# Reordering the opening of a beacon-attention and maxout-FFN kernel: other places for the first loads, casts, masks and copies

## The chip, the cores and the metric

The kernel runs on one core of a Trainium2 chip. A core has five engines, each with its own instruction queue that is worked off in order: TensorE (PE, matrix multiplies and transposes), VectorE (DVE), ScalarE (ACT), GpSimd (POOL) and SyncE (SP, which here only asks for transfers). Transfers between device memory and the on-chip memory (SBUF) run on 16 DMA engines, fed by a queue for each engine that asks: SyncE's, ScalarE's and GpSimd's. TensorE writes to PSUM, from which the other engines copy to SBUF. The metric is the device time in microseconds of one execution.

## The reference

The inputs are q, k and v of 8 batches, 8 heads, 576 positions and 64 dimensions, 16 further "beacon" keys and values for each batch and head, three weights of 512 x 768 and one of 768 x 512, all float32.

```python
k_all = concat([beacon_k, k]);  v_all = concat([beacon_v, v])
scores = (q @ k_all.T) / 8, causal for the ordinary keys, beacons always seen
a = softmax(scores);  attn = a @ v_all
x = attn as [4608 tokens, 512]
h = maximum(maximum(x @ w1, x @ w2), x @ w3)
out = h @ w_out
```

## The kernel before

The work on the attention goes by pairs of heads (four a batch, 32 in all); a "quad" is two pairs. For a pair the queries and keys are turned by TensorE so that the 64 dimensions lie on partitions (queries in `qT`, keys behind 16 beacon columns in `kT`). Keys and values are cut into five tiles of 128 rows, the first with the beacons in its first 16 rows. Scores are computed with keys on partitions, in four groups a pair (`emit_scores`, L503 to L525: matmuls at L514, an exponential by ScalarE at L523). The causal triangle is put to zero afterwards (`emit_masks`): by GpSimd with a select (L542), or by VectorE with a product with the constant `tri` (L540), which GpSimd makes in the step `triangle` (L787, L788). `emit_pv` (L583) multiplies with ones, for the sums, and with the values, for a quad and half of the positions at a time. ScalarE inverts the sums (`invert`), and VectorE multiplies into `xT` (`multiply`, L616).

The FFN of the first 512 tokens runs in half units of 8 matmuls (`mm1_halves`, L638); VectorE copies the first result (L630) or takes the maximum (L632). The step `("ffn", bank, kind)` takes the next half unit of tokens 0 to 255 (kind 0) or 256 to 511 (kind 1), in the order first, second, third weight, three units each. A bank is one of two in `ffn_psum`, one of two in `pv_psum`, or one from a ring of score tiles, which has two places and from the step `widen` on three. A later user of a place waits until the earlier one is emptied.

The order of all work is written out by hand: the list `first_steps` (L901) for the opening, and `loop_steps` after it. Each step appends its instructions to the queues of the engines that it uses, so the list fixes the order on each engine, and engines run against each other by semaphores alone. Steps that matter here:

- `busy n cols`: n spare matmuls on constants (L478). Spare work is also given with `scores` (third number) and `half` (spare transposes, L408).
- `load half p i queue` (L223): queries (i = 0) or keys (i = 1) of the first half of the positions of pair p of batch 0, asked for by the queue named. `cast half` (L231) makes them bf16 on the engine named.
- `load keys 0` (L351): the beacon keys of batch 0. `cast keys 0`, then `turn keys 0` (L360, copies at L366 and L367), then `keys p engine` (L460), which copies the beacon columns of pair p into `kT`.
- `load quad half g h` (L240): queries and keys of half h of quad g of batch 0, as bf16, from GpSimd's queue. `load quad b g` (L249): a whole quad of batch b in the same way. `load w i` (L338): weight i, two transfers from the same queue.
- `half p h ...` (L440, copies at L448) and `whole p ...` (L389, copies at L464 and L453): turn the queries and then the keys of a pair. Pairs from 8 on come in float32 (`load pair`, L206), are cast by GpSimd (`cast pair`, L259) and turned at L398.
- `load v0 t [gate]`: value tile t of batch 0 (L276, L279), asked for by SyncE. `load v b piece [gate]`: three or two tiles of a later batch. With a gate the engine named first writes one element of the tile (L301, L295; L202 for pairs), and SyncE waits for that. `cast v0 t engine` (L328) and `cast v b piece` (L316, GpSimd) make them bf16.

On GpSimd's queue the requests for transfers, the casts, the selects and the small writes stand behind one another, so a request goes out only when all that was listed ahead of it is done. On SyncE a request whose gate is not yet written holds up those behind it.

## Time and profile before

| | us |
|---|---|
| three runs | 284.79, 285.10, 286.19 (median 285.1) |
| the profiled execution's own time | 285.21 |
| its span, first to last instruction | 283.3 |
| busy: TensorE, VectorE, ScalarE, GpSimd | 276.3, 176.5, 154.5, 143.4 |

The mean clock granted to TensorE is 0.998 of full. In the rows of the profile, a line "Lnnn engine operation out<-in" is a group of instructions of one line of the code; in rows ordered by time the first number is the start and the second the length, both in microseconds from the start of the span, and a bracket gives the idle time before the group and what ended it. `quad`, `whole` and `h` are the staged queries and keys, `bk` the beacon keys, `st` the float32 stage of values and pairs, `at_sb` the exponentials. "issue" is time in which the engine waited for nothing that the profile shows.

### The profile page before, as it was taken

How to read it: one execution, taken by the hardware profiler on the slowest of the kernel's cores; microseconds unless marked ns; L12 is line 12 of the kernel's file. 1: busy time of each engine (PE TensorE's matmuls, PEld its weight loads, DVE VectorE, ACT ScalarE, POOL GpSimd, SP SyncE). 2: the span in 40 equal slices, each digit the busy share in tenths (PEclk: the TensorE clock that was granted, in tenths of full speed). 3: DMA queues.
4: the chain of work that ended last, by engine and by line, in shares of the span. 5: the costliest groups of instructions: out<-in, count | busy, mean ns of one | idle time of the engine just before them, and what ended most of it. 6: DMA issues, size and time to landing. Idle time of an engine off the chain costs nothing.

```text
span 283.3 us, 11781 instructions
## 1 busy us (share of the span) xinstructions
PE 276.3 (98%) x5099; PEld 201.5 (71%) x5099; DVE 176.5 (62%) x331; ACT 154.5 (55%) x249; POOL 143.4 (51%) x316
## 2 busy tenths in 40 slices
PE   8999999999999999999999999999999999999995
PEld 7666777757777576768677686767877687757762
DVE  2456777886676765756566666646575665661754
ACT  2876676897563574637464574725765474624000
POOL 4462318898741583758734497508854682400000
PEclk9999999999999999999999999999999999999999
DMA  9999999999978399999999969989999962003004
GB/s 153 168 171 206 223 234 157 247 206 309 211 141 168 45 252 178 171 197 147 189 178 215 236 91 176 166 204 185 217 160 170 163 177 76 2 3 150 2 2 185
DMA packets 118307, 46.27 MB, mean 163 GB/s; under 512 B 107248, under 2 KB 112880, under 8 KB 118256
## 3 DMA queue, kind: packets, MB, share of 16 engines
q1 hardware_dynamic: 111888, 39.20, 75.6%
q0 software_dynamic: 5808, 6.00, 13.0%
q8 instruction: 40, 0.66, 1.1%
q10 hardware_dynamic: 560, 0.33, 0.4%
q14 instruction: 11, 0.09, 0.1%
HBM read 35.13 MB, written 9.44 MB: 157 GB/s over the span
## 4 chain that ended last, share of the span: by engine, by line
PE 91%; DMA 3%; ACT 2%; POOL 1%; DVE 1%; issue 1%; ACTq 0%; POOLq 0%
PE t L700 44%; PE t L726 16%; PE t L583 11%; PE t L514 6%; DMA quad<-in_k_dram 3%; PE pv L478 2%; ACT at_sb L523 2%; PE pv L638 2%; PE sc L514 1%; PE sc L638 1%; PE fps L638 1%; PE t L398 1%; POOL at_sb L542 1%; PE wide L583 1%; PE pv L583 1%
## 5 line engine op out<-in xcount | busy, mean ns | idle before, releaser
L700 PE MATMUL t<-xT,w_sb 64*128 64x288 bf16 (+1 forms) x1008 | 129.6, 285 | 0.0
L700 PE MATMUL t<-xC,wC 64*128 64x288 bf16 (+1 forms) x1008 | 129.6, 285 | 0.0
L523 ACT ACTIVATE at_sb<-t 128x992 bf16<-128x992 f32 (+1 forms) x96 | 82.6, 863 | 42.8 <-PE t L514 37.1
L632 DVE TENSOR_TENSOR hT<-hT,t 128x576 bf16<-128x576 bf16 (+1 forms) x84 | 63.7, 763 | 30.6 <-PE t L700 30.6
L542 POOL TENSOR_SCALAR_AFFINE_SELECT at_sb<-at_sb 128x256 bf16<-128x256 bf16 (+2 forms) x143 | 53.6, 390 | 53.7 <-ACT at_sb L523 41.2
L700 PEld LDWEIGHTS <-w_sb 64*128 64x128 bf16 x1008 | 51.3, 94 | 12.6 <-issue 1.1
L700 PEld LDWEIGHTS <-wC 64*128 64x128 bf16 x1008 | 51.0, 94 | 12.4
L726 PE MATMUL t<-w_out_sb,hT 128*128 128x512 bf16 x210 | 47.9, 380 | 0.0
L681 POOL COPY xC<-xT 64x576 bf16<-64x576 bf16 (+1 forms) x26 | 18.0, 693 | 42.8 <-DVE xT L616 42.5
L630 DVE CAST hT<-t 128x576 bf16<-128x576 f32 (+1 forms) x36 | 27.7, 769 | 14.8 <-PE t L700 14.6
L726 PEld LDWEIGHTS <-hT 128*128 128x128 bf16 x210 | 19.3, 98 | 22.8 <-issue 0.9
L259 POOL CAST p<-st 96x768 bf16<-96x768 f32 x44 | 34.9, 822 | 0.3
L734 DVE COPY y<-t 128x1024 f32<-128x1024 f32 (+1 forms) x20 | 21.8, 1091 | 20.5 <-PE t L726 20.3
L514 PE MATMUL t<-qT,kT 64*128 64x288 bf16 (+4 forms) x288 | 33.1, 279 | 0.0
L616 DVE TENSOR_TENSOR xT<-t,recip 128x288 bf16<-128x288 f32 (+2 forms) x78 | 22.9, 351 | 16.0 <-ACT recip L606 10.7
L604 ACT ACTIVATE lnd<-t 128x288 f32<-128x288 f32 x26 | 10.7, 410 | 36.9 <-PE t L583 36.9
L514 PEld LDWEIGHTS <-kT 64*128 64x128 bf16 x400 | 18.5, 94 | 11.4 <-issue 6.7
L583 PEld LDWEIGHTS <-v_sb 128*32 128x32 bf16 (+1 forms) x1408 | 24.6, 96 | 1.6 <-issue 0.4
L523 ACT ACTIVATE at_sb<-sc 128x736 bf16<-128x736 f32 (+5 forms) x28 | 23.2, 862 | 4.2 <-PE sc L514 4.1
L583 PE MATMUL t<-at_sb,v_sb 128*32 128x96 bf16 (+8 forms) x1144 | 23.3, 228 | 0.0
L316 POOL CAST v_sb<-st 128x1536 bf16<-128x1536 f32 (+2 forms) x21 | 18.4, 894 | 0.6 <-DMA st<-in_v_dram 0.6
L583 PEld LDWEIGHTS <-ones 128*32 128x32 bf16 (+2 forms) x512 | 10.9, 95 | 6.7 <-issue 3.9
(125 smaller groups left out, 220.1 us busy)
## 6 DMA issues: line engine op xcount, KB each, us to landing
out_dram<-y SPq DMA_DIRECT2D x15, 512.0 KB, 4.6
st<-in_q_dram SPq DMA_DIRECT2D x24, 288.0 KB, 5.8
st<-in_k_dram SPq DMA_DIRECT2D x24, 288.0 KB, 6.2
st<-in_v_dram SPq DMA_DIRECT2D x24, 256.0 KB, 5.5
w_sb<-in_moe_w_dram POOLq DMA_DIRECT2D x6, 384.0 KB, 8.9
st<-in_v_dram SPq DMA_DIRECT2D x8, 224.0 KB, 5.1
st<-in_v_dram SPq DMA_DIRECT2D x8, 160.0 KB, 4.7
out_dram<-y SPq DMA_DIRECT2D x5, 256.0 KB, 4.6
```

The lines of the kernel that those rows point to most:

```text
L259: cast(t16.rearrange("p r h d -> p h r d"), st[0:QP, i * NQ2 : (i + 1) * NQ2].rearrange("p (h r d) -> p h r d", h=2, r=QR),)
L316: cast(v_sb[0:n, t:t1].rearrange("p t h d -> p (t h d)"), st[0:n, (t - t_lo) * H * D : (t1 - t_lo) * H * D],)
L514: nc.tensor.matmul(ps[:, e, off : off + q1 - q0], kT[hs, 128 * t : 128 * t + 128], qT[hs, q0:q1], start=True, stop=True, tile_position=(64 ...
L523: nc.scalar.activation(out=both_heads(p, gi), in_=ps[:, :, 0 : g_width(p, gi)], func=AF.Exp, scale=scale)
L542: nc.gpsimd.affine_select(out=view, in_=view, compare_op=ALU.is_ge, fill=0.0, base=x0, pattern=[[0, 2], [1, hi - lo]], channel_multiplier=-1,)
L583: nc.tensor.matmul(ps[bank][32 * j : 32 * j + 32, lo + q0 - qa : lo + qb - qa], lhsT, at_view(PPQ * quad + j // 2, t, j % 2, q0, qb), star ...
L616: nc.vector.tensor_mul(xT[:, 2 * g + part - 1, c0 + ca : c0 + cb], ps[bank][:, lo : lo + cb - ca], recip[:, ca:cb],)
L630: (by_i or by_dve)(h, ps)
L632: nc.vector.tensor_max(h, h, ps)
L700: nc.tensor.matmul(ps[:, e], w[own(e), ct, cols], x, start=(ct == 0 and not over), stop=(ct == n_ct - 1 and over), tile_position=(64 * e, 0),)
L726: nc.tensor.matmul(ps[:, u], h_tile(tt + u, ft), w_out_sb[:, ft, :], start=(ft == 0), stop=(ft == n_ft - 1),)
L734: nc.vector.tensor_copy(y[:, 0:n], ps[:, 0:n])
```

## The change

Only the list `first_steps` is changed; the functions stay as they are. What moves:

- The two `busy` blocks change places. The request for quad half (1, 0) goes out ahead of the `triangle`, which goes behind the copy of the beacon columns of pair 3, and so ahead of the request for quad half (0, 1).
- The beacon keys are asked for ahead of the keys of pair 0 in ScalarE's queue, and ScalarE casts the queries of pair 0 ahead of the beacon keys.
- The value tiles of batch 0 are asked for in the order 0, 2, 1, all three gated by GpSimd. Tile 0 (before: GpSimd) and tiles 2 and 3 (before: ScalarE) are cast by VectorE.
- The turn of pair 2 goes ahead of that of pair 3, and `scores 1 0` behind both; the turn of the second half of pair 1 goes ahead of `scores 0 1`. Two spare matmuls go (`scores 0 2` and `scores 1 2` have 3 instead of 4).
- Masks 3 0 and 3 1 go from VectorE to GpSimd, masks 0 2, 4 3 and 5 1 from GpSimd to VectorE; the copies `keys 4` go from GpSimd and `keys 7` from ScalarE to VectorE.
- The second and third weights are asked for later in GpSimd's queue: the second behind mask 0 1, the third behind mask 3 2. Quad (1, 0) thereby goes ahead of the third weight and quad (1, 1) behind masks 3 1 and 2 2.
- The first values of batch 1 are asked for after the fourth FFN unit, and pair 8 before `scores 4 1`.
- One FFN unit of kind 0 and some score groups change places around the turn of pair 6, which goes ahead of an FFN unit and of `scores 5 3`.
- In the last part the steps `keys 8`, `keys 9`, `mask 6 0` and two score groups move by a few places.

```diff
@@ -899,176 +899,176 @@
         "cast keys 2": lambda e: by[e](bk16, bk32),
     }
     first_steps = [
+        ("busy", 16, 160),
         ("load half", 0, 0, "sp"),
+        ("identity",),
+        ("load quad half", 1, 0),
         ("busy", 27, 200),
-        ("identity",),
-        ("busy", 16, 160),
-        ("triangle",),
-        ("load quad half", 1, 0),
         ("load half", 1, 0, "act"),
+        ("load keys 0", "act"),
+        ("cast half", 0, 0, "act"),
+        ("cast half", 1, 0, "pool"),
         ("load half", 0, 1, "act"),
         ("cast half", 0, 1, "dve"),
-        ("load keys 0", "act"),
         ("cast keys 0", "act"),
         ("load half", 1, 1, "sp"),
-        ("cast half", 0, 0, "act"),
         ("turn keys 0",),
-        ("cast half", 1, 0, "pool"),
         ("load v0", 0, "pool"),
         ("cast half", 1, 1, "dve"),
+        ("load v0", 2, "pool"),
         ("load v0", 1, "pool"),
         ("half", 0, 0, "ffn", "act", 0, 8),
         ("keys", 1, "act"),
-        ("load v0", 2),
+        ("keys", 3, "pool"),
+        ("triangle",),
         ("half", 1, 0, "pv", "act", 3, 5),
-        ("keys", 3, "pool"),
         ("load quad half", 0, 1),
         ("scores", 0, 0, 0),
-        ("scores", 1, 0, 0),
+        ("cast v0", 0, "dve"),
+        ("half", 2, 0, "pv", "dve", 4, 0),
         ("load w", 0),
         ("half", 3, 0, "ffn", "dve", 0, 0),
-        ("half", 2, 0, "pv", "dve", 4, 0),
+        ("scores", 1, 0, 0),
         ("mask", 1, 0, "dve"),
-        ("cast v0", 0, "pool"),
         ("cast v0", 1, "act"),
+        ("mask", 0, 0, "dve"),
         ("scores", 3, 0, 0),
-        ("mask", 0, 0, "dve"),
-        ("load v0", 3, "dve"),
         ("keys", 2, "pool"),
-        ("cast v0", 2, "act"),
+        ("cast v0", 2, "dve"),
         ("scores", 2, 0, 7),
         ("values", 0, 0, "pv", 0, 4, 0),
+        ("load v0", 3, "dve"),
         ("half", 0, 1, "ffn", "act", 0, 9),
         ("invert",),
-        ("mask", 3, 0, "dve"),
+        ("load keys 1",),
+        ("mask", 3, 0, "pool"),
         ("multiply",),
-        ("scores", 0, 2, 4),
+        ("scores", 0, 2, 3),
         ("mask", 2, 0, "pool"),
-        ("load keys 1",),
         ("scores", 0, 3, 0),
         ("values", 1, 0, "ffn", 0, 4, 0),
         ("load quad half", 1, 1),
         ("invert",),
+        ("half", 1, 1, "pv", "act", 1, 0),
         ("multiply",),
-        ("mask", 0, 2, "pool"),
+        ("mask", 0, 2, "dve"),
+        ("load v0", 4, "dve"),
         ("scores", 0, 1, 0),
-        ("half", 1, 1, "pv", "act", 1, 0),
-        ("load v0", 4, "dve"),
-        ("scores", 1, 2, 4),
+        ("scores", 1, 2, 3),
+        ("cast v0", 3, "dve"),
         ("mask", 0, 1, "pool"),
-        ("cast v0", 3, "act"),
         ("ffn", "ring", 0),
         ("ffn", "ffn", 0),
         ("mask", 1, 2, "dve"),
         ("scores", 1, 3, 0),
         ("scores", 1, 1, 0),
+        ("mask", 1, 3, "dve"),
         ("half", 2, 1, "pv", "dve", 0, 0),
-        ("mask", 1, 3, "dve"),
+        ("mask", 0, 3, "dve"),
         ("ffn", "ffn", 0),
         ("half", 3, 1, "pv", "dve", 0, 0),
-        ("load v", 1, 0, "dve"),
         ("cast v0", 4, "dve"),
-        ("mask", 0, 3, "dve"),
         ("mask", 1, 1, "dve"),
         ("scores", 2, 3, 0),
         ("scores", 2, 2, 7),
         ("load w", 1),
+        ("cast keys 1", "dve"),
         ("scores", 3, 2, 0),
         ("mask", 2, 3, "dve"),
-        ("cast keys 1", "dve"),
         ("values", 0, 1, "pv", 0, 4, 0),
+        ("invert",),
         ("turn keys 1",),
-        ("invert",),
         ("scores", 3, 3, 0),
         ("ffn", "ffn", 0),
+        ("load v", 1, 0, "dve"),
+        ("scores", 2, 1, 0),
         ("load quad", 1, 0),
-        ("load w", 2),
         ("mask", 3, 3, "dve"),
         ("multiply",),
         ("load pair", 9, "pool"),
-        ("scores", 2, 1, 0),
+        ("mask", 3, 2, "pool"),
+        ("load w", 2),
+        ("mask", 2, 1, "pool"),
+        ("keys", 5, "dve"),
+        ("ffn", "ffn", 0),
+        ("scores", 3, 1, 0),
+        ("mask", 3, 1, "pool"),
         ("mask", 2, 2, "pool"),
-        ("ffn", "ffn", 0),
-        ("mask", 2, 1, "pool"),
-        ("scores", 3, 1, 0),
+        ("ffn", "ring", 0),
+        ("whole", 4, "ffn", "dve"),
         ("keys", 6, "dve"),
-        ("keys", 4, "pool"),
-        ("ffn", "ring", 0),
-        ("mask", 3, 1, "dve"),
-        ("keys", 5, "dve"),
-        ("mask", 3, 2, "pool"),
-        ("whole", 4, "ffn", "dve"),
         ("values", 1, 1, "pv+", 0, 4, 0),
-        ("invert",),
+        ("load pair", 8),
+        ("invert",),
+        ("keys", 4, "dve"),
         ("scores", 4, 1, 0),
         ("multiply",),
         ("widen",),
         ("scores", 4, 2, 0),
         ("whole", 5, "ring", "act"),
-        ("load pair", 8),
         ("ffn", "ring", 1),
         ("mask", 4, 1, "dve"),
         ("ffn", "ring", 1),
         ("scores", 5, 0, 0),
+        ("scores", 4, 3, 0),
+        ("ffn", "pv", 1),
+        ("scores", 4, 0, 0),
+        ("load v", 1, 1),
+        ("scores", 5, 2, 0),
+        ("ffn", "pv", 1),
         ("mask", 5, 0, "dve"),
-        ("ffn", "pv", 1),
-        ("load v", 1, 1),
-        ("scores", 4, 0, 0),
-        ("scores", 4, 3, 0),
+        ("load quad", 1, 1),
         ("ffn", "ring", 0),
-        ("ffn", "pv", 1),
-        ("load quad", 1, 1),
         ("mask", 4, 2, "dve"),
         ("scores", 5, 1, 0),
-        ("keys", 7, "act"),
-        ("scores", 5, 2, 0),
+        ("keys", 7, "dve"),
+        ("whole", 6, "ring", "act"),
+        ("ffn", "pv", 0),
         ("scores", 5, 3, 0),
-        ("mask", 4, 3, "pool"),
-        ("ffn", "pv", 0),
-        ("whole", 6, "ring", "dve"),
         ("cast v", 1, 0),
         ("mask", 5, 3, "pool"),
+        ("mask", 4, 3, "dve"),
+        ("mask", 5, 2, "pool"),
+        ("ffn", "ring", 0),
         ("load w_out", "pool"),
         ("mask", 4, 0, "pool"),
-        ("ffn", "ring", 0),
-        ("mask", 5, 2, "pool"),
         ("ffn", "pv", 1),
         ("scores", 6, 1, 0),
         ("scores", 6, 0, 0),
-        ("mask", 5, 1, "pool"),
+        ("mask", 5, 1, "dve"),
         ("scores", 6, 2, 0),
         ("ffn", "pv", 1),
         ("whole", 7, "ring", "dve"),
+        ("mask", 6, 0, "pool"),
         ("load", 2, "dve"),
         ("values", 2, 0, "ring", 0, 4, 0),
         ("load", 1, "pool"),
-        ("mask", 6, 0, "pool"),
         ("load", 2, "pool"),
         ("ffn", "pv", 1),
         ("invert",),
         ("multiply",),
-        ("keys", 8, "pool"),
+        ("cast pair", 8),
         ("load", 1),
-        ("cast pair", 8),
         ("cast v", 1, 1),
         ("scores", 6, 3, 0),
-        ("scores", 7, 2, 0),
-        ("cast pair", 9),
+        ("scores", 7, 1, 0),
+        ("keys", 9, "act"),
         ("whole", 8, "pv", "dve"),
         ("mask", 6, 3, "dve"),
         ("scores", 7, 0, 0),
-        ("scores", 7, 1, 0),
+        ("keys", 8, "pool"),
+        ("cast pair", 9),
+        ("scores", 7, 2, 0),
         ("mask", 7, 1, "pool"),
         ("values", 2, 1, "ring", 0, 4, 0),
         ("mask", 7, 2, "pool"),
         ("invert",),
         ("scores", 7, 3, 0),
-        ("whole", 9, "ring", "act"),
         ("mask", 6, 1, "pool"),
         ("mask", 7, 3, "pool"),
+        ("whole", 9, "ring", "act"),
         ("multiply",),
         ("mask", 7, 0, "pool"),
-        ("keys", 9, "act"),
         ("ffn", "pv", 1),
         ("mask", 6, 2, "pool"),
     ]
```

## The prediction

> **What bounds the kernel now.** I read the page first. One execution's span is 283.3 us and its own time 285.21 us, so 1.91 us lie around the span; I sum against 285.21. The median of the three runs shown is 285.1, which is 0.11 less.

> ```profile
> span 283.3 us, 11781 instructions
> ...
> PE 276.3 (98%) x5099; PEld 201.5 (71%) x5099; DVE 176.5 (62%) x331; ACT 154.5 (55%) x249; POOL 143.4 (51%) x316
> ```

> TensorE is busy in 98% of the span, so after the opening every microsecond that TensorE loses stays lost, and nothing else can gain. Then I read busy time by stretches of 5 us (the columns are the stretch, its length, TensorE, weight loads, VectorE, ScalarE, GpSimd, granted clock, DMA share, GB/s).

> ```profile
> 20.00:25.00 5.00, 4.44 (x57) 3.12 (x56) 3.37 (x8) 2.67 (x5) 2.94 (x6) 1.00 0.98 183
> ```

> TensorE idles 0.56 us of the stretch shown, with the clock granted in full (1.00) and the DMA engines loaded all the time (0.98). The gaps that count are few; the chain of work that ended last (start, length, what) names them.

> ```profile
> 15.65 7.10 DMA quad<-in_k_dram
> ...
> 22.79 0.32 PE pv L440 x6
> ...
> 32.45 0.20 DVE at_sb L540
> 32.66 0.16 DVE kT L460
> ...
> 34.07 0.36 issue
> ...
> 41.67 0.14 PE wide L514 x2
> 41.81 0.98 PE pv L638 x8
> 42.79 0.63 PE sc L389 x24
> ...
> 48.48 0.14 POOL kT L460
> ...
> 50.20 0.43 PE pv L398 x6
> ```

> Three waits stand in it. At 22.79 TensorE has been waiting for the second-half keys of heads 4 to 7, a transfer asked for from GpSimd's queue at 15.65. At 34.07 it waits for VectorE's copies of pair 4. At 50.20 it waits for GpSimd, which writes beacon columns (48.48) ahead of the casts of pair 8. Everything before 22.79 can therefore only be felt through that transfer, or by making TensorE arrive after it.

> **The change part by part: up to 23 us.**

> ```profile
> 1.34 5.86 PE L478 MATMUL pv<-busy 128*128 128x200 bf16 x43 [1.34 <-DVE busy L138]
> ...
> 17.93 0.72 PE L478 MATMUL sc<-busy 128*128 128x320 bf16 x4
> 19.20 0.34 PE L514 MATMUL sc<-qT,kT 64*128 64x288 bf16 x4 [0.56 <-ACT qT L448]
> ...
> 23.04 1.05 PE L638 MATMUL fps<-xT,w_sb 128*128 128x256 bf16 x8
> ```
> ```profile
> 6.25 0.62 ACT L864 CAST bk<-bk 16x512 bf16<-16x512 f32 x1 [4.15 <-DMA bk<-in_beacon_k_dram]
> ...
> 21.41 0.62 ACT L328 CAST v_sb<-st 128x512 bf16<-128x512 f32 x1 [1.06 <-DVE hT L630]
> ```
> ```profile
> 5.70 0.63 DVE L231 CAST h<-h 96x384 bf16<-96x384 f32 x2 [3.89 <-DMA h<-in_k_dram]
> ...
> 20.70 0.69 DVE L630 CAST hT<-sc 128x512 bf16<-128x512 f32 x1 [1.33 <-PE sc L638]
> ...
> 25.69 0.42 DVE L328 CAST v_sb<-st 80x512 bf16<-80x512 f32 x1
> ```

> The two blocks of spare matmuls change places but not number: 43 in 5.86 us, then the turn of the beacon keys at 7.2. Beacon keys second instead of third in ScalarE's queue land before 6.25, and the query cast of some 0.5 us goes into ScalarE's idle 4.15 us, so both are ready by 7.2 as before. The keys of pair 0 move to third place; VectorE cast them at 5.70, half a microsecond later is still early, since TensorE takes them after the beacons and the queries. All of this I cost at nothing; its cover is the spare block, and without that it would be worth about 0.4 us.

> ```profile
> 4.90 8.19 SPq L279 DMA_DIRECT2D st<-in_v_dram  x4
> ```
> ```profile
> st<-in_v_dram SPq DMA_DIRECT2D x1, 224.0 KB, 4.7
> ```

> The first value tile is requested at 4.90 and lands 4.7 us later, at 9.6. VectorE now has its cast (0.42 us by the row at 25.69) ahead of the copies of pairs 2 and 3, so they and `scores 3` come up to 0.6 us later. ScalarE loses one value cast. The half-turn of pair 1 goes ahead of `scores 0 1`, which removes the 0.56 us wait at 19.20, and two spare matmuls of 0.72 / 4 = 0.18 us (about 0.13 us apart) go. These gains and losses of 0.3 to 0.6 us all lie before the wait at 22.79, which hides them: nothing, with +0.6 and -0.85 as ends.

> What reaches 22.79 is two things. First, VectorE now casts value tile 3 before it empties the first FFN bank. ScalarE could start that cast only at 21.41 after 1.06 us of idleness; the FFN work named as releaser has nothing to do with it, so I read it as the tile's landing. Then 21.41 + 0.42 (cast) + 0.69 (the emptying, the row at 20.70) = 22.52, after which TensorE still has `scores 1 1` (some 0.3 us) and two half turns (some 0.3 us): 23.15 to 23.2 for the third FFN unit, which started at 23.04. Second, GpSimd's queue:

> ```profile
> 1.32 0.20 POOL L787 MEMSET tri<- 128x128 bf16 x1
> 1.60 0.29 POOL L788 TENSOR_SCALAR_AFFINE_SELECT tri<-tri 128x128 bf16<-128x128 bf16 x1
> ...
> 8.33 0.67 POOL L240 DMA_DIRECT2D quad<-in_q_dram  x1 [0.28 <-issue]
> ```

> The triangle's two instructions (0.20 + 0.29 us) go behind the beacon columns and ahead of the request at 8.33, of which the 0.28 us of idleness may cover part. GpSimd's transfers then run one after another to the landing at 22.75 (15.65 + 7.10), so that comes 0.2 to 0.5 us later; the quad request that moves 0.5 us forward at the start gives perhaps 0.2 back. The removed VectorE mask of pair 3 goes to GpSimd, in a gap in which it waits for ScalarE. Ends for this stage: -0.3 and +0.5; I take **+0.25**, between the two routes.

> **From 23 to 60 us.** The later request of whole heads 4 to 7 (batch 1, second group) is the largest term.

> ```profile
> 30.66 0.41 POOL L542 TENSOR_SCALAR_AFFINE_SELECT at_sb<-at_sb 128x256 bf16<-128x256 bf16 x1 [3.43 <-ACT at_sb L523]
> ...
> 31.16 0.32 POOL L542 TENSOR_SCALAR_AFFINE_SELECT at_sb<-at_sb 80x160 bf16<-80x160 bf16 x1
> 31.43 0.70 POOL L249 DMA_DIRECT2D whole<-in_q_dram  x1
> ...
> 41.99 1.47 POOL L316 CAST v_sb<-st 128x1536 bf16<-128x1536 f32 x1 [0.59 <-DMA st<-in_v_dram]
> ```
> ```profile
> 30.79 1.00 ACT L523 ACTIVATE at_sb<-sc 128x992 bf16<-128x992 f32 x1 [0.19 <-PE sc L514]
> ```
> ```profile
> whole<-in_k_dram POOLq DMA_DIRECT2D x1, 288.0 KB, 9.9
> ```

> Before, it stood behind a mask that ran at 31.16, and went out at 31.43 and 0.70 later. Now GpSimd first makes mask 3 1 (0.41 us), which needs the exponential that ends at 30.79 + 1.00 = 31.79, and then mask 2 2 (0.32): 31.79 + 0.25 + 0.41 + 0.32 = 32.8, less some overlap, 1.3 us later. The keys' half landed at 32.12 + 9.9 = 42.0; now at 43.3. Its user is the turn of pair 6 at 42.79, which moves ahead of one FFN unit (0.98) and one score pair (0.14): it begins at 42.79 - 1.12 = 41.67, its keys 0.31 later, with the 0.25 from above at 42.2. So the slack of 1.1 us becomes a wait of 1.1 us. Is the transfer bound by its request or by the third weight ahead of it? In 33 to 34 us the GpSimd queue moved this much:

> ```profile
> q0 software_dynamic: 15, 0.04, 21.2%
> ```

> Its transfers took a fifth of the engines' time, so the queue was nearly empty and the request decided. The weight itself is asked for after mask 3 2, six microseconds later, but still two to three before the queue runs out, and its first use comes one unit later: nothing, as long as that backlog covers it; without it up to 1 us. Ends for this term: 0 (weight still in the way in some rings until the old time) and 1.9 (the later transfer also shares with the pair loads); I take **+1.1**, nearer the row of the near-empty queue.

> At 34.07 the mask (0.20) and one beacon copy (0.16) leave VectorE's chain, two beacon copies and a gate of some 0.06 come in behind the turn: 0, ends -0.3 and +0.1. The beacon copy of pair 8 goes behind the casts: **-0.14** from the row at 48.48. `keys 7`, masks 4 3 and 5 1 go to VectorE, where TensorE does not wait; their cover is VectorE's idle time, and without it 0.2 to 0.4 each.

> The values of batch 1 are gated on VectorE some four microseconds later (behind the fourth FFN unit instead of the third; 4.2 by the order of VectorE's work, an estimate). In 25.7 to 28 us, after the request, the two queues moved (packets, MB, share):

> ```profile
> q0 software_dynamic: 561, 0.44, 124.0%
> ...
> q1 hardware_dynamic: 11, 0.00, 0.9%
> ```

> The value loads got 11 packets out of 572, so asking then brought nothing; I cost the later request at 0, with 41.99 as the cast's time still.

> [...]

> Sum: 285.21 + 0.25 + 1.1 - 0.14 = **286.4 us**. That is 0.4% over the median; half a percent, 1.4 us, is about what a measurement of this kernel can tell from no change.

> **The rivals.** *The late transfer is not late.* If the third weight is what held the queue until 34 us or later, the same time is kept, the wait at pair 6 is 0 to 0.3, and the time is 285.4. For it: the key half took 9.9 us in all. Against: the near-empty queue. 0.2.

> *Faster.* The opening's transfers may land earlier, as the quad request goes out 0.5 us sooner. If the landing at 22.75 comes 0.6 us sooner, the idle 0.56 us goes, with the spares (0.27) and the reordered half turn already saved TensorE keeps up, and with no wait at pair 6 the time is 285.21 - 0.56 - 0.27 - 0.14 - 0.3 (34.07) = 283.9. It decides once value tile 3 also lands before 20.8. Against: GpSimd's queue gets the triangle. 0.12.

> *Values of batch 1 late.* Between the cast at 41.99 and `values 2 0` GpSimd has four more masks to make:

> ```profile
> 45.50 1.37 POOL L542 TENSOR_SCALAR_AFFINE_SELECT at_sb<-at_sb 128x224 bf16<-128x224 bf16 x4
> ```
> ```profile
> 47.48 0.41 PE L583 MATMUL sc<-at_sb,ones 128*32 128x288 bf16 x12
> ```

> They end at 46.87, 0.6 us ahead of the values at 47.48. With TensorE itself 1.1 later and one of the four masks gone to VectorE (1.37 / 4 = 0.34), the last tile may land as late as 41.99 + 0.6 + 1.1 + 0.34 = 44.0. If it lands by as much later as its gate opens, 41.99 + 4.2 = 46.2, TensorE waits 2.2 us more: 288.6. For it: the cast at 41.99 already waited 0.59. Against: the 11 packets. 0.1.

> *VectorE's casts hold GpSimd up.* A mask of 0.41 us took 1.12 beside VectorE's SBUF copies:

> ```profile
> 57.77 1.12 POOL L542 TENSOR_SCALAR_AFFINE_SELECT at_sb<-at_sb 128x256 bf16<-128x256 bf16 x1
> ```
> ```profile
> 56.59 2.04 DVE L670 COPY wC<-w_sb 64x3072 bf16<-64x3072 bf16 x2
> ```

> If the new cast on VectorE (0.42) does the same to the requests that go out beside it at 9 to 11 us, all of GpSimd's transfers come that much later: 286.8. For it: these two rows. Against: it needs exact coincidence, and the queue has a backlog soon after. 0.08. [...]

> **How the numbers follow.** My forecast, a wait at pair 6 of 0.4 to 1.9 us, has 0.5, its own range 285.7 to 287.3. Slower by over 0.5% means above 286.5: nearly half of my forecast's case (0.24), the late values (0.1), most of the lockout (0.06): 0.4. Faster by over 0.5% means under 283.7: a good half of the faster case, whose 283.9 can come out lower by the spread of its transfers, 0.08. The rest, 0.52, is within. The range reaches from the faster rival to a landing of the values half a microsecond short of the slow one, 283.9 to 288.1.

> **What would show it.** In the profile after: the third FFN unit of block 0 starting near 23.3; VectorE's cast of value tile 3 waiting for its transfer until about 21.4; the request of the second whole quad near 32.7 and its keys landing near 43.3; TensorE idle by about 1 us in the middle of the turn of pair 6, released by that transfer; the cast of batch 1's values still at about 42; pair 8 turned without the 0.14. The prediction is wrong if the turn of pair 6 doesn't wait, if TensorE idles more than 0.5 us anywhere in 24 to 41 us, or if GpSimd's cast starts after 44.0.

## The result and the profile after

The kernel after takes 289.03 us (median of 8 runs, 286.11 to 291.4), beside 285.31 for the kernel before: a ratio of 1.0101 with a 95% interval of 1.0059 to 1.0143. It is slower by 1%, and it spreads wider than before. The ratio is under that of the two medians, 1.013, because it compares means and leaves out one slow run, that of 291.4 us (mean clock 0.994). A second set of runs on another occasion (e4 below) gave 1.0102 [1.0074, 1.013]. The profiled execution took 287.6 us, 1.4 under that median, so its trace shows a favourable case; it is 2.4 us over the profiled 285.21 of before.

The page of the kernel after begins with the span and the busy times; the last line is the DMA queue of kind "instruction", which brings the program itself (packets, MB, share).

```profile
span 285.8 us, 11756 instructions
...
PE 275.6 (96%) x5083; PEld 201.1 (70%) x5097; DVE 177.1 (62%) x334; ACT 154.5 (54%) x247; POOL 144.2 (50%) x316
...
q8 instruction: 40, 0.66, 1.1%
```

TensorE does the same work (275.6 us busy instead of 276.3) in a span that is 2.5 us longer. So the loss is waiting. What TensorE waits for, by line (us in total, times, longest), in the kernel after:

```profile
PE pv L478 <- DVE busy L138: 1.3, 1, 1.3
PE fps L440 <- DVE h L231: 0.9, 1, 0.9
PE sc L514 <- DVE kT L448: 0.8, 1, 0.8
PE sc L638 <- ACT at_sb L523: 0.8, 2, 0.6
PE t L514 <- DMA kT<-p: 0.7, 1, 0.7
PE pv L398 <- POOL p L259: 0.6, 2, 0.3
PE t L583 <- issue: 0.5, 1, 0.5
PE sc L583 <- POOL at_sb L542: 0.2, 1, 0.2
```

And in the kernel before:

```profile
PE pv L478 <- DVE busy L138: 1.3, 1, 1.3
PE sc L514 <- DVE kT L448: 0.7, 2, 0.5
PE pv L440 <- DMA quad<-in_k_dram: 0.6, 1, 0.6
PE sc L514 <- ACT qT L448: 0.6, 1, 0.6
PE sc L514 <- DVE qT L453: 0.4, 1, 0.4
```

These lines add up to 5.8 us after and 3.6 before, 2.2 more. With the hole of 0.27 us in the turn of pair 6, shown next, that is about the 2.5 us of the span.

The places in the kernel after, in order of time (start, length, what, idle time before it and its releaser):

```profile
3.93 0.51 ACT L231 CAST h<-h 96x384 bf16<-96x384 f32 x1 [1.84 <-DMA h<-in_q_dram]
3.94 0.32 ACTq L223 DMA_DIRECT2D h<-in_k_dram  x1
8.17 0.62 DVE L231 CAST h<-h 96x384 bf16<-96x384 f32 x2 [6.36 <-DMA h<-in_k_dram]
8.59 0.32 PE L440 MATMUL fps<-ident,h 96*64 96x96 bf16 x6 [0.85 <-DVE h L231]
...
21.20 0.43 DVE L328 CAST v_sb<-st 128x512 bf16<-128x512 f32 x1 [1.13 <-DMA st<-in_v_dram]
...
33.30 0.68 POOL L249 DMA_DIRECT2D whole<-in_k_dram  x1
41.46 0.96 PE L389 MATMUL wide<-ident,whole 96*64 96x96 bf16 x24
44.06 1.60 POOL L316 CAST v_sb<-st 128x1536 bf16<-128x1536 f32 x1 [10.08 <-DVE kT L464]
...
50.56 0.43 PE L398 MATMUL pv<-ident,p 96*128 96x96 bf16 x6 [0.30 <-POOL p L259]
51.33 0.43 PE L398 MATMUL pv<-ident,p 96*128 96x96 bf16 x6 [0.34 <-POOL p L259]
...
58.06 0.43 PE L583 MATMUL t<-at_sb,v_sb 128*32 128x48 bf16 x23 [0.50 <-issue]
```

Read from the top: ScalarE's cast of the queries of pair 0 waits for their landing at 3.93, and the request for the keys of pair 0 stands behind it in the same queue, so it goes out at 3.94 (1.29 before); VectorE casts the keys at 8.17 (5.70 before) and TensorE waits 0.85 us. VectorE waits 1.13 us for value tile 3. The turn of pair 6 takes 0.96 us, where the same 24 matmuls take 0.70 without a wait: a hole of about 0.27. GpSimd casts the values of batch 1 2.1 us later than before (44.06 beside 41.99; the bracket names VectorE, but the third tile landed only at 43.86), and the two halves of the turn of pair 8 wait for its casts. At 58.06 TensorE stands still for 0.50 us, and nothing in the profile releases it.

By milestones the two profiled runs differ like this: first FFN unit 20.15 (before 19.47), third 23.22 (23.04), seventh 35.55 (35.69), first of the values of batch 1 48.02 (47.48). At the first matmul of line 700 (66.39, before 64.72) the difference is 1.7 us, and the wait for a transposing transfer of keys near 229 us adds 0.7. So in this run the whole loss comes after 41 us. The experiments show that in other runs it comes elsewhere.

### The profile page after: what moved, and what is told of

Same layout as the page of the kernel before. It is cut to its first block, busy times and chain, and to the rows that moved or that the text cites. A ratio compares the mean times of both kernels' runs of the same rounds, so it can differ in the third digit from the quotient of the medians.

```text
span 285.8 us, 11756 instructions
## 1 busy us (share of the span) xinstructions
PE 275.6 (96%) x5083; PEld 201.1 (70%) x5097; DVE 177.1 (62%) x334; ACT 154.5 (54%) x247; POOL 144.2 (50%) x316
## 4 chain that ended last, share of the span: by engine, by line
PE 85%; DMA 8%; POOL 2%; DVE 1%; issue 1%; ACT 1%; SPq 0%; ACTq 0%; POOLq 0%
PE t L700 43%; PE t L726 16%; PE t L583 11%; PE t L514 6%; DMA quad<-in_k_dram 2%; DMA st<-in_k_dram 2%; DMA kT<-p 1%; DMA h<-in_k_dram 1%; PE sc L514 1%; PE pv L638 1%; PE pv L583 1%; DMA h<-in_q_dram 1%; PE fps L638 1%; PE sc L638 1%; ACT at_sb L523 1%
## 5 line engine op out<-in xcount | busy, mean ns | idle before, releaser
L523 ACT ACTIVATE at_sb<-t 128x992 bf16<-128x992 f32 (+1 forms) x96 | 82.7, 864 | 43.6 <-PE t L514 38.5
L542 POOL TENSOR_SCALAR_AFFINE_SELECT at_sb<-at_sb 128x256 bf16<-128x256 bf16 (+2 forms) x144 | 54.2, 393 | 45.8 <-ACT at_sb L523 42.6
L726 PE MATMUL t<-w_out_sb,hT 128*128 128x512 bf16 x196 | 47.2, 380 | 0.7
L630 DVE CAST hT<-t 128x576 bf16<-128x576 f32 (+1 forms) x36 | 27.7, 769 | 15.7 <-PE t L700 15.4
L726 PEld LDWEIGHTS <-hT 128*128 128x128 bf16 x210 | 19.4, 98 | 22.8 <-issue 1.0
L734 DVE COPY y<-t 128x1024 f32<-128x1024 f32 (+1 forms) x20 | 21.8, 1091 | 21.2 <-PE t L726 21.0
L514 PE MATMUL t<-qT,kT 64*128 64x288 bf16 (+4 forms) x288 | 33.1, 279 | 0.7 <-DMA kT<-p 0.7
L514 PEld LDWEIGHTS <-kT 64*128 64x128 bf16 x400 | 18.1, 94 | 12.0 <-issue 5.0
L523 ACT ACTIVATE at_sb<-sc 128x992 bf16<-128x992 f32 (+5 forms) x28 | 23.2, 860 | 5.6 <-PE sc L514 5.4
L583 PEld LDWEIGHTS <-v_sb 128*32 128x32 bf16 (+1 forms) x1408 | 24.5, 96 | 2.4 <-issue 1.0
L583 PE MATMUL t<-at_sb,v_sb 128*32 128x96 bf16 (+8 forms) x1144 | 23.5, 228 | 0.5 <-issue 0.5
L316 POOL CAST v_sb<-st 128x1536 bf16<-128x1536 f32 (+2 forms) x21 | 18.5, 901 | 10.1 <-DVE kT L464 10.1
L638 PEld LDWEIGHTS <-w_sb 128*128 128x128 bf16 x144 | 13.2, 98 | 4.0 <-issue 2.2
## 6 DMA issues: line engine op xcount, KB each, us to landing
st<-in_q_dram SPq DMA_DIRECT2D x24, 288.0 KB, 5.7
st<-in_k_dram SPq DMA_DIRECT2D x24, 288.0 KB, 6.0
st<-in_v_dram SPq DMA_DIRECT2D x8, 224.0 KB, 5.2
```

Source lines behind the costliest of these rows:

```text
L514: nc.tensor.matmul(ps[:, e, off : off + q1 - q0], kT[hs, 128 * t : 128 * t + 128], qT[hs, q0:q1], start=True, stop=True, tile_position=(64 ...
L523: nc.scalar.activation(out=both_heads(p, gi), in_=ps[:, :, 0 : g_width(p, gi)], func=AF.Exp, scale=scale)
L542: nc.gpsimd.affine_select(out=view, in_=view, compare_op=ALU.is_ge, fill=0.0, base=x0, pattern=[[0, 2], [1, hi - lo]], channel_multiplier=-1,)
L583: nc.tensor.matmul(ps[bank][32 * j : 32 * j + 32, lo + q0 - qa : lo + qb - qa], lhsT, at_view(PPQ * quad + j // 2, t, j % 2, q0, qb), star ...
L630: (by_i or by_dve)(h, ps)
L638: nc.tensor.matmul(ps[:, f], w_in[i][:, ct, 128 * (ft + f) : 128 * (ft + f + 1)], xT[:, ct, lo : lo + MID], start=(ct == 0), stop=(ct == n ...
```

## The experiments

The list has 172 steps in both kernels, and after 63, 107 and 144 steps both have issued the same set of work. So the list can be divided there and put together from both; the first two fences of edits below are written as slices of the two lists. All ratios are to the kernel before, measured beside it.

| run | edit | median us | ratio, 95% interval |
|---|---|---|---|
| e4_after_again | the kernel after | 288.76 | 1.0102 [1.0074, 1.013] |
| e1_opening | only steps 1 to 63 of after | 286.96 | 1.0049 [1.0026, 1.0071] |
| e2_middle | only steps 64 to 107 | 286.59 | 1.0039 [1.0019, 1.0059] |
| e3_last | only steps 108 to 172 | 287.14 | 1.0049 [1.0029, 1.0069] |
| e5_third | only steps 108 to 144 | 286.6 | 1.0039 [1.0018, 1.006] |
| e6_fourth | only steps 145 to 172 | 285.84 | 1.0001 [0.9983, 1.0019] |
| e7_k0_first | e1, keys of pair 0 asked for first | 287.43 | 1.0061 [1.0034, 1.0087] |
| g1_opening_two | e7, tile 3 cast by ScalarE | 286.85 | 1.0048 [1.003, 1.0065] |
| f4_tile3_alone | before, tile 3 cast by VectorE | 285.65 | 1.0022 [0.9996, 1.0049] |
| e9_quad_early | e2, second quad asked for earlier | 285.91 | 1.002 [0.9994, 1.0046] |
| f1_tile3 | after, tile 3 cast by ScalarE | 288.51 | 1.0135 [1.0092, 1.0178] |
| f2_pair6 | after, both edits at pair 6 undone | 287.61 | 1.0067 [1.0042, 1.0092] |
| f3_three | f1 and f2 and e7 together | 286.56 | 1.0041 [1.0011, 1.007] |
| g2_four | f3, last part as before | 287.52 | 1.0075 [1.005, 1.0099] |
| g3_after_blocks | after, 36 instructions fewer at the start | 290.56 | 1.0164 [1.0137, 1.019] |
| g4_before_blocks | before, 36 fewer | 287.43 | 1.0067 [1.0044, 1.0091] |
| h1_before_plus | before, 20 more | 285.44 | 1.0 [0.9971, 1.0029] |
| h2_after_plus | after, 24 more | 289.57 | 1.011 [1.0076, 1.0144] |

### Which part of the list costs

```diff
-first_steps = before[0:172]
+first_steps = after[0:63] + before[63:172]      (e1_opening)
+first_steps = before[0:63] + after[63:107] + before[107:172]      (e2_middle)
+first_steps = before[0:107] + after[107:172]      (e3_last)
+first_steps = after[0:172]      (e4_after_again)
```

> Only the first 63 steps in the new order (to the scores of pair 1, some 22 us), the rest as before. Theory A, the transfers asked for later between 23 and 34 us cost the time: here +0.2 us, since TensorE's third FFN unit started at 23.22 against 23.04 in the two profiles, so about 285.5. Rival B, the opening costs it (the keys of pair 0 are now requested only at 3.94 us, behind ScalarE's cast, and TensorE idled 0.85 and 0.82 us): all later transfers shift and the time is about 288 to 289.

> Only steps 64 to 107 in the new order (from the half turn of pair 2 to the turn of pair 5: third weight, values of batch 1 and second whole quad asked for later), the rest as before. Theory A: most of the loss, 287.5 to 289, with GpSimd's cast of the values of batch 1 starting near 44 us instead of 42. Rival B: within 0.3 us of before. Rival C, the new order of the last part is the cause: within 0.5 us of before.

> Only steps 108 to 172 in the new order (the turn of pair 6 ahead of an FFN unit, GpSimd's masks and casts between 40 and 60 us in another order), the rest as before. Theory A and rival B: within 0.3 us of before, the casts of pair 8 a little earlier. Rival C: 287 or more, GpSimd's later masks late from 45 us on.

> The changed kernel once more, beside the three parts on the same chip. All theories: 287 to 291, some 1% over the kernel before. If the parts add up, its loss is the sum of theirs; if it is larger, they work on one another.

Each of the three parts costs 0.4 to 0.5%, so no theory that puts the loss into one part survives. The sum of the three, 1.37%, is over the 1.02% of the whole, but the intervals leave room for the two to be equal. In the middle alone TensorE waits where the prediction said:

```profile
44.06 0.45 PE L389 MATMUL sc<-ident,whole 96*64 96x96 bf16 x12 [1.44 <-DMA whole<-in_k_dram]
```

TensorE stands 1.44 us in the turn of pair 6 until the keys of the second whole quad have landed. This part holds only one of the two moves that the forecast of 1.1 us put together, the later request. The keys were asked for at 32.90, 0.78 us later than in the kernel before (32.12), and landed at 44.01, 2.0 later (41.98): the transfer itself took 11.1 us instead of 9.9, so the later request does not account for all of the wait. The values of batch 1, whose loads are also asked for later in this part, are cast at 40.80 in this run, earlier than the 41.99 of before: here their later request costs nothing. The second set of runs of the kernel after has nearly the median of the first, but its profile has other holes:

```profile
37.08 0.39 PE L514 MATMUL sc<-qT,kT 64*128 64x80 bf16 x3 [1.15 <-issue]
60.91 0.43 PE L583 MATMUL t<-at_sb,v_sb 128*32 128x48 bf16 x23 [0.69 <-issue]
```

TensorE waits 1.06 us for the keys of pair 0, 1.08 us for the second half of the second weight, 1.15 and 0.69 us without a releaser, and not at all at pair 6.

The last part was then cut once more.

```diff
+first_steps = before[0:107] + after[107:144] + before[144:172]      (e5_third)
+first_steps = before[0:144] + after[144:172]      (e6_fourth)
```

> The order of before with only the stretch from the second ring unit of block 1 to the values of batch 1 (34 to 47 us) taken from the kernel after. Theory S3: the 0.49% of the last part sits here, because GpSimd's masks 5 3 and 4 0 and the casts behind them run later, so that the values of batch 1 wait about 0.2 us and the turn of pair 8 waits for GpSimd's casts: 286.3 to 286.9. Theory S4: this stretch costs nothing and the turn of pair 8 keeps before's wait: 285.2 to 285.6.

> The order of before up to the gate of the value loads at 47 us, and only what follows (beacon keys 8 behind the casts of pairs 8 and 9, order of scores 7) from the kernel after. My prediction priced this at -0.14: 285.1. Theory S4: the order of the casts and of keys 8 on GpSimd is what makes the turn of pair 8 wait, 0.3 us or more longer than before: 286.0 to 286.9. Theory S3: 285.1 to 285.5. If TensorE's stall that the trace ends by nothing but its own issue (at about 58 us, values 3 0) shows here, it goes with this part; if it shows in the run of the third stretch, with that.

The third stretch carries the cost, the fourth none. In the third alone the turn of pair 6, which stands ahead of an FFN unit there, waits for the same keys with the early request:

```profile
42.92 0.45 PE L389 MATMUL wide<-ident,whole 96*64 96x96 bf16 x12 [1.14 <-DMA whole<-in_k_dram]
58.86 0.47 PE L583 MATMUL t<-at_sb,v_sb 128*32 128x176 bf16 x23 [1.13 <-issue]
```

So an earlier turn (e5) and a later request (e2) each let TensorE wait at pair 6, where the prediction had found a slack of about 1 us. The casts for pair 8 are late only with the third and fourth part together: from the sixteenth to the seventeenth FFN unit, which hold the turn of pair 8, the profiled runs of before, e5 and e6 need 5.34, 5.33 and 5.31 us, those of e3 and after 5.77 and 5.79. That is 0.45 us more; before's 5.34 already holds a wait of about 0.25 us in the same turn. The hole at 58 us shows in the fourth part too (1.20 us in the profiled run of e6_fourth) although that part costs nothing in the median.

### What of the opening costs

```diff
+("load half", 0, 1, "act"),
 ("cast half", 0, 0, "act"),
 ("cast half", 1, 0, "pool"),
-("load half", 0, 1, "act"),
```

> The opening alone of the kernel after, with one thing undone: the keys of pair 0 are requested on ScalarE's queue ahead of ScalarE's query cast, as before, still behind the beacon keys. Theory K (the request stood behind the cast, which waits for its own transfer, and cost 2.65 us on the request and 0.85 us on TensorE): the wait for VectorE's cast at 8.6 us is gone, 285.3 to 285.7. Rival (the opening loses by its other edits: value tiles cast by VectorE, triangle on GpSimd, longer rings): no change from the opening alone, 286.7 to 287.1.

The wait at 8.6 us is gone in e7, as expected, and the time is not: 1.0061. The next step of the same kind came forward.

```profile
22.73 0.43 DVE L328 CAST v_sb<-st 128x512 bf16<-128x512 f32 x1 [3.06 <-DMA st<-in_v_dram]
23.81 0.39 PE L514 MATMUL sc<-qT,kT 64*128 64x288 bf16 x4 [1.41 <-DVE hT L630]
```

VectorE idles 3.06 us because the head of its queue is the cast of value tile 3, which lands at 22.7 in this run; the emptying of the FFN bank stands behind it, and TensorE waits 1.41 us for that. The landing is not the same from run to run: in the kernel after the cast began at 21.20, in f2_pair6 at 22.28, in e4 the tile was there when VectorE came at 20.55. So tile 3 was tried both ways: moved alone, and undone in the kernel after and in the opening.

```diff
-("load v0", 3, "dve"),
 ("values", 0, 0, "pv", 0, 4, 0),
+("load v0", 3, "dve"),
...
-("cast v0", 3, "act"),
+("cast v0", 3, "dve"),
```

This is the edit of f4. In f1 and g1 only the engine of the cast goes back to ScalarE.

> The kernel before with one part of the change alone: the fourth value tile of batch 0 is gated behind the first values and cast by VectorE instead of ScalarE. Theory V: TensorE waits 0.5 to 1.5 us for VectorE's emptying near 23 us in part of the runs, part of it in place of the 0.56 us that before waits for the quad keys there: 285.8 to 286.8. Rival: the wait for the quad keys hides it, 285.2 to 285.6.

> The kernel after with one edit undone: the fourth value tile of batch 0 (cast v0 3) is cast by ScalarE again. Theory V (VectorE stands waiting for that tile's landing, with the emptying of the first FFN bank queued behind it, and TensorE waits 1.4 us for it in the two opening runs where the tile landed at 22.8): 0.7 to 1.3 us under the kernel after, 287.5 to 288.2. Rival (the opening loses in the k0 wait and the ring alone, the tile's landing is noise): 288.6 to 289.1.

> The opening alone of the kernel after with two things undone: keys of pair 0 requested ahead of ScalarE's cast, and the fourth value tile cast by ScalarE. Theory O (each of the two is a chance of a wait of about 1 us, the later one with a half-speed clock behind it in part of the runs; undoing one leaves the other): 285.3 to 285.9, no wait of TensorE for VectorE near 24 us, and no run with a granted clock under 0.997. Rival (what is left of the opening, the longer way of the first turned keys and the triangle, costs the 0.5%): 286.5 to 287.3.

Alone it costs 0.22%, with an interval that includes no change (f4). Undone in the kernel after it brings nothing that can be told (f1), and undone together with the request of the keys it still leaves 0.48% for the opening (g1): the expectation that these two are the whole opening is wrong. The profile of g1 shows a third wait of the same form.

```profile
9.34 0.43 DVE L328 CAST v_sb<-st 128x512 bf16<-128x512 f32 x1 [0.80 <-DMA st<-in_v_dram]
11.37 0.61 PE L514 MATMUL sc<-qT,kT 64*128 64x288 bf16 x6 [1.71 <-DVE kT L448]
```

Here it is value tile 0: VectorE waits for its landing with the copies of pairs 2 and 3 behind it. Every profile with the opening of after has at least 0.81 us of wait at this place, where before has 0.20 and 0.46: in ten of the eleven it is 0.81 to 0.88, some 0.2 us more than before's two together, and 1.71 only in g1. In g1 this wait costs more than its length. The busy times by stretches of g1 (stretch, length, TensorE, weight loads, VectorE, ScalarE, GpSimd, granted clock, DMA share, GB/s):

```profile
9.60:11.30 1.70, 0.06 (x4) 0.00 (x0) 1.70 (x6) 1.02 (x1) 1.03 (x3) 1.00 1.51 198
11.30:14.70 3.40, 3.33 (x27) 1.64 (x27) 1.32 (x8) 1.70 (x3) 0.31 (x1) 0.50 1.10 149
14.70:16.00 1.30, 1.30 (x48) 0.77 (x42) 0.00 (x0) 0.87 (x1) 1.00 (x5) 0.99 0.95 174
```

After these 1.7 us without work TensorE's clock was granted at 0.50 for 3.4 us, which is another 1.7 us lost in this run.

### Pair 6

```diff
 ("mask", 2, 1, "pool"),
+("load quad", 1, 1),
 ("keys", 5, "dve"),
...
-("load quad", 1, 1),
```

> The middle alone of the kernel after, with the request of the second whole quad put ahead of masks 3 1 and 2 2 on GpSimd, at about 31.1 us instead of 32.2. Theory Q (the later request is the loss): the wait of 1.44 us in the turn of pair 6 falls to 0.3 or less, 285.2 to 285.6. Rival (the transfer is late for another reason: the third weight, asked for 5 us later, is still in GpSimd's queue ahead of it): the wait stays at 1 us or more, 286.3 to 286.8.

The wait of 1.44 us is gone from the turn of pair 6 with the request back in its place, and the ratio is 1.002 instead of 1.0039. The two intervals overlap, and that of e9 includes no change, so how much of the cost went with the wait is not shown; e9's profiled run lost 1.01 us earlier, at the quad keys near 23 us, and 0.94 us at 58 us. In the kernel after both edits at pair 6 were undone, and then the edits of the opening with them:

```diff
 ("mask", 2, 1, "pool"),
+("load quad", 1, 1),
...
-("load quad", 1, 1),
...
-("whole", 6, "ring", "act"),
 ("ffn", "pv", 0),
 ("scores", 5, 3, 0),
+("whole", 6, "ring", "act"),
 ("cast v", 1, 0),
```

> The kernel after with both edits around pair 6 undone: the second whole quad is requested behind mask 2 1, at about 31.3 us, and pair 6 is turned behind the FFN unit again. Theory P (the later request of e2 and the earlier turn of e5 each eat the same slack of about 1 us, and waits of 1.44 and 1.14 us stood there): 0.8 to 1.5 us under the kernel after, 287.3 to 288.0. Rival (in the kernel after TensorE already arrives late enough, its profile has only 0.27 us of wait there): 288.6 to 289.1.

> The kernel after with three things undone: keys of pair 0 requested ahead of ScalarE's cast, fourth value tile cast by ScalarE, both edits around pair 6. If theories V, P and the request of k0 together are the cause, it stands within 0.3% of before: 285.0 to 286.3. If the loss lies in what is left (value loads of batch 1 asked for later, GpSimd's masks later, third weight later, triangle), it stays above 287.

> The kernel after with four things undone: the three of the run before and, on GpSimd, beacon keys 8 and the casts of pairs 8 and 9 as well as the score order of pair 7 as in the kernel before. Theory C (moving keys 8 behind the casts costs nothing while GpSimd is early, as in the run of the fourth part alone, but 0.3 to 0.45 us once the third stretch has made GpSimd late): 0.3 to 0.5 us under the run with three undone, 285.7 to 286.3, and the turn of pair 8 waits for GpSimd by 0.2 us or less. Rival: no difference to the run with three undone, 286.3 to 286.9.

Undoing the two edits at pair 6 gives 1.0067 (f2) beside 1.0102 for the kernel after; the two were measured on different occasions and their intervals overlap, so a gain of 0.35%, 1.0 us, is likely and not shown. With the two of the opening undone as well it is 1.0041 (f3), whose interval lies wholly under that of the kernel after in e4: the three together give back some 0.6%. That is a little above what was expected if these were all. The fourth edit (g2: the last 28 steps as before) does its work on the spot, from the sixteenth to the seventeenth FFN unit its profiled run needs 5.34 us as before, but the total gives nothing back, 1.0075: its profile has a stall of 1.30 us near 58 us, of the kind of the next part. The difference between f3 and g2, whose intervals overlap, is not understood.

### The stalls without a releaser

Where TensorE stands still and the profile names only its own issue, the place in any one kernel is one of two instructions of its program, and these are 768 instructions apart, three times 256. The page of the kernel after counts 40 packets and 0.66 MB in the queue of the program, 16.5 KB each. TensorE's 5,097 weight loads have a matmul each, of which the trace lacks 14, so 10,194 instructions: about 255 a packet. Theory, from these two counts: a packet is a block of 256 instructions, and the stall is the next block of the program arriving late. The test moves the block limits and leaves the work nearly the same: the spare columns at the start in fewer, wider matmuls (8,000 columns for 7,960), or in more and narrower ones (5,402 and 5,382 for 5,400).

```diff
-("busy", 16, 160),
+("busy", 8, 320),
-("busy", 27, 200),
+("busy", 17, 320),      (g3 and g4; h1: 37 of 146, h2: 39 of 138, the 16 of 160 kept)
```

> The kernel after with the same spare work at the start cut into fewer, wider matmuls (8 of 320 columns for 16 of 160, 17 of 320 for 27 of 200): 36 instructions fewer ahead of everything else. Theory I (TensorE's stalls that nothing but its own issue ends are the arrival of the next 16 KB block of its program, every 256 instructions): a stall near 58 us, if there is one, now stands 36 instructions later, at a matmul of 96 columns of the same values instead of one of 48, and one near 34 to 37 us in the turn of a pair instead of the scores; total unchanged to 1 us lower. Rival (the stall belongs to that matmul or to the accumulation bank it writes): it stays at the same matmul of the values.

> The kernel before with the same cut of the spare work, 36 instructions fewer ahead of everything else. Theory I: the stall of 0.23 to 0.36 us at 34 us leaves the first scores of pair 4 and stands elsewhere or nowhere; between 284.6 and 285.8. Rival: it stays in front of the scores of pair 4, whose copies it waits for.

In g3 both stalls stand where the theory puts them, 36 instructions later, in the turn of a pair and at a matmul of 96 columns, and they are long:

```profile
38.14 0.37 PE L389 MATMUL wide<-ident,whole 96*64 96x96 bf16 x9 [2.98 <-issue]
63.81 0.23 PE L583 MATMUL t<-at_sb,v_sb 128*32 128x96 bf16 x5 [2.35 <-issue]
```

The DMA queues of g3 between 35.8 and 37.0 us (packets, MB, share of 16 engines) hold the block:

```profile
q0 software_dynamic: 110, 0.09, 62.5%
q1 hardware_dynamic: 338, 0.08, 44.0%
q8 instruction: 1, 0.02, 4.9%
```

In the five microseconds ahead, from 30.9, when TensorE began the block before, that queue moved nothing, while the two data queues (q0 and q1) took 74.7% and 35.2% of the time of the 16 engines. The block's transfer starts at 35.91, and TensorE goes on at 38.14. The kernel before with the same cut lost 0.67%, with the stall at the predicted matmul:

```profile
57.16 0.25 PE L583 MATMUL t<-at_sb,v_sb 128*32 128x96 bf16 x8 [0.84 <-issue]
```

That much is shown in g3: with the block's transfer begun only at 35.91 and 61.20, TensorE stood for 2.98 and 2.35 us, at the places that the block limits give. What it costs in the median is not. g3 was forecast at no change or up to 1 us less and came at 290.56 beside 288.76; g4 was forecast at 284.6 to 285.8 and came at 287.43. The profile of g4 is its fastest run (285.79), so the stalls of its other runs were not seen, and the wider spare matmuls themselves may have a part in both losses. Is a late block also a reason for the difference between the two kernels? For that the limits were moved the other way, to where the shortest block lasts longer.

> The kernel before with the first spare work cut the other way, 37 matmuls of 146 columns for 27 of 200: 20 instructions more ahead of everything else, so that the limits of the program blocks fall 20 instructions earlier. By the trace of before the seventh block would then take 5.5 us instead of 5.1 and the one that ends near 34 us 5.9 instead of 5.8, and the shortest of all is 5.0 instead of 4.2 us. Theory I: the stalls near 34 and 57 us are rarer, 0 to 1.2 us under before, 284.2 to 285.5. Rival (the 0.67% of the other cut came from the wider spare matmuls themselves, through the clock or the first turns): no gain, 285.3 to 287.

> The kernel after with 39 spare matmuls of 138 columns for 27 of 200: 24 instructions more. By the trace of after the shortest block is then 5.0 us instead of 3.7. Theory I as a cause of part of the loss (two spare matmuls fewer and the new order put the block limits badly): 0.8 to 1.5 us under the kernel after, 287.2 to 288.2. Rival (block limits play no part in the difference between the two kernels): 288.5 to 289.2.

Neither gains: 1.0 for the kernel before, 1.011 for the kernel after. The 285.44 of h1 lies in the range of the theory and in that of its rival, and the 289.57 of h2 above the 288.2 that the theory allowed. No stall of this kind is left in the profile of h2, and TensorE is at the seventh FFN unit at 35.83. Then it stands at pair 6:

```profile
44.69 0.45 PE L389 MATMUL wide<-ident,whole 96*64 96x96 bf16 x12 [2.50 <-DMA whole<-in_k_dram]
```

```profile
42.20:44.70 2.50, 0.01 (x2) 0.01 (x2) 1.14 (x3) 0.43 (x1) 0.91 (x1) 1.00 1.10 247
44.70:46.00 1.30, 1.30 (x20) 1.00 (x20) 0.76 (x1) 0.03 (x1) 0.00 (x0) 1.00 1.20 223
46.00:49.50 3.50, 3.50 (x19) 2.31 (x18) 1.57 (x3) 1.27 (x2) 1.85 (x5) 0.51 0.73 100
```

The wait of 2.50 us is followed by 3.5 us at half the clock. So a block stall ahead of pair 6 may be no loss of its own: it delays TensorE and can cover the wait there. The profiles fit that in part: e4 has a stall of 1.15 us near 37 us and no wait at pair 6, f1 and h2 have no stall there and wait 2.22 and 2.50 us. But the first profile of the kernel after has no stall there either and waits only 0.27, and a stall near 58 us comes too late to cover anything at pair 6. It is argued, then, and not shown. Seven of the eleven runs of h2 have a mean clock of 0.994 or less; of the 20 runs of the kernel after only two have 0.994, so a half clock is not what makes its median slower.

## Why the prediction was wrong

I forecast 286.4 with a range of 283.9 to 288.1; 289.03 lies outside. Slower by over 0.5% had 0.4, and within 0.5% had 0.52.

The step that failed first is the opening. Up to 23 us the sum had +0.25; alone it costs 0.49%, 1.4 us (e1). The term of pair 6 failed next: the middle and the last part had +0.96 together (1.1 less 0.14), and alone they cost 0.39% and 0.49%, 1.1 and 1.4 us. The whole is 1.02%, 2.9 us, where the sum had 1.2. What in these parts costs the time is shown for about 0.6% of it, which three edits undone together bring back (f3); the rest stays open.

**Up to 23 us, the step costed at nothing.** I wrote that the keys of pair 0 come "half a microsecond later", since they move to third place in their queue. They also move behind a cast on ScalarE, and the request went out behind that cast, at 3.94 instead of 1.29: 2.65 us later, a wait of 0.85 us in the profiled run, none in e1 and 0.23 to 1.43 us in the other profiles with this order. The keys land between 8.0 and 8.6 us in all of them; the wait differs with when the spare matmuls ahead are done (the turn of the beacon keys starts at 6.89 in after and at 7.98 in e1). The diff had the line; I counted the DMAs and not the cast between them.

**Up to 23 us, the casts on VectorE.** Both were seen (tile 0 ahead of the copies, tile 3 ahead of the emptying), and the arithmetic for tile 3 was right for this run: VectorE's cast at 21.20 (forecast 21.4), the third FFN unit at 23.22 (forecast near 23.3, so +0.18 for +0.25). What failed is the single landing behind it. The tile lands anywhere from before 20.6 to 22.7, and the price is then 0 to 1.4 us. For tile 0 I had called the wait at 22.79 the cover; it covers 0.56 us, and the new wait behind tile 0 was 0.81 to 0.88 in most profiles and 1.71 in g1.

**The turn of pair 6.** The mechanism was right where the wait appears, and its numbers were near: request at 32.62 (forecast 32.7), and the keys landed between 41.9 (33.30 + 8.6) and 44.7 (33.6 + 11.1 in h2), with 43.3 forecast. Against 1.1 forecast the wait was nothing in e4, 0.27 in the first profile of the kernel after, 1.44 in e2, 2.22 in f1 and 2.50 in h2. Undoing both edits came out at 0.35%, 1.0 us, less, which would be near the forecast but is not clear of the noise. Two things were missing: the spread of the landing, and that TensorE is itself delayed ahead of the turn, so that the same landing is late in one run and not in the next. In f1 and h2 a half clock stands with the wait as well (0.50 from 44.16 to 50.99 in f1, 0.51 from 46.0 to 49.5 in h2).

**Pair 8, forecast at -0.14.** The beacon copy was not what pair 8 waited for but the start of GpSimd's casts: moving the copy alone gave 5.31 us for 5.34 between the two FFN units (e6). With the third and fourth part together the value cast, the last weight and four masks come later on GpSimd (casts of pair 8 from 49.68, before 48.55), and the turn waits 0.30 + 0.34 us. With the third part alone it does not wait longer than before (e5).

**The 0 at 34.07.** I read the 0.36 us of "issue" there as VectorE's copies. The weight loads of the kernel before say otherwise:

```profile
34.11 0.09 PEld L514 LDWEIGHTS <-kT 64*128 64x128 bf16 x1 [0.24 <-DVE qT L453]
34.44 0.23 PEld L514 LDWEIGHTS <-kT 64*128 64x128 bf16 x5 [0.23 <-issue]
34.44 0.53 PE L514 MATMUL sc<-qT,kT 64*128 64x288 bf16 x6 [0.42 <-DVE qT L453]
```

The copies release the first weight load at 34.11. The first matmul, at 34.44, is by the count the first instruction of a program block, the one whose limit g3 and g4 moved, and the second weight load stands right behind it. The block's transfer began at 32.16, 2.28 us before. It was a term with the wrong cause, and the sum took no price for the blocks at all.

**The values of batch 1.** The later request was costed at nothing, with the cast still at 42. e2 bears that out (third tile landed at 38.88, cast at 40.80), the kernel after does not: there the third tile was asked for at 32.28 and landed at 43.86, and the cast began at 44.06, past the 44.0 that the prediction named as a sign of being wrong; in e4 it began at 44.56. TensorE waited only 0.23 us for these values, and e3, with the early request and the cast at 40.99, has a wait of 0.19 there too. So the forecast of the landing failed, but it is not where the time went, and the rival of late values (cast at 46.2) did not happen. The 561 packets against 11 were misread: in that stretch the value loads had hardly begun, since SyncE's queue started to move data at 29.2, 3.5 us after the request. From 30.40 to 31.20 in e3, where both queues had work, they moved 60 and 59 packets:

```profile
q0 software_dynamic: 60, 0.15, 95.3%
q1 hardware_dynamic: 59, 0.02, 13.2%
```

Of the other rivals, the late transfer that is not late fits the profiled run (0.27 us) and not e2 or h2. VectorE's casts did not hold GpSimd up: the first weight was asked for at 9.69, before at 9.65.

**The range.** All prices came from one profiled run. In the changed order four transfers (queries of pair 0, value tiles 0 and 3, the second whole quad) have an engine waiting with other work behind; for the last two the landings could be compared, and they spread by at least 2.1 and 2.5 us. A sum of one landing each has no such spread.

**What stays open.** With three edits undone 0.4% are left (f3), and in the opening 0.5% with two undone (g1). Value tile 0 on VectorE is a candidate for the latter, argued from the wait of 1.71 us in one profile and not tried by itself; in most profiles that wait is only some 0.2 us longer than before's. What makes the second whole quad land after 8.6 us in one run and after 11.1 in another was not found. No version was faster than the kernel before; h1_before_plus (1.0) and e6_fourth (1.0001) equal it within their intervals.

## What to carry to other kernels

For each step that a change moves, ask what stands at the head of an in-order queue and whether it waits for a transfer: here a request behind a cast went out 2.65 us later, and a cast ahead of copies held VectorE for 3.06 us (e7), and one trace shows only one landing. Where an engine is busy for 96 to 98% of the time, as TensorE here, waits may cover each other (argued at pair 6, not shown), and undoing one cause may bring nothing until the next is undone too (e7, with the request of the keys put back, came at 1.0061 beside 1.0049); price them together, and by several profiles. A wait of TensorE is to be priced with its clock (1.71 us in g1, then 3.4 us at 0.50), and a hole that the profile gives to "issue" may be the program itself arriving late (2.98 us in g3).

## What the runs showed of the hardware

**TensorE's program came in packets of about 255 instructions, and a late one stopped TensorE.** The queue of the program moved 40 packets and 0.66 MB in the kernel after, in 1.1% of the time of the 16 DMA engines. TensorE went on 2.2 to 2.8 us after the start of the packet's transfer in these stalls: 35.91 to 38.14 and 61.20 to 63.81 in g3, 55.46 to 58.06 in the kernel after, 56.1 to 58.81 in e3, 34.8 to 37.08 and 58.1 to 60.91 in e4. The transfer started up to 5.0 us after TensorE had entered the block before (30.93 to 35.91 in g3); the work of that block was done at 35.16, 0.75 us ahead of the transfer, and TensorE stood until 38.14, for 2.98 us.

**Waits of 1.59 to 2.98 us were followed by half the clock of TensorE, but one of 2.35 us was not.** After 1.71 us of idleness in g1 and 2.50 us in h2 the granted clock was about 0.5 for 3.4 and 3.5 us; after 1.41 and 1.44 us (e7, e2) it stayed at 1.00. But it stayed so after 2.35 us in g3 too, so the length of the wait alone did not decide. In the clock of g3 by 40 slices of 7.26 us, the only dip is the one behind its wait of 2.98 us, at 38.7:

```profile
PEclk9999979999999999999999999999999999999999
```
